# The fourth product of a maximum's scores with 64 rows instead of 32

## The chip, the cores and the metric

One core of one Trainium2 chip runs the whole program. The metric is the device time of one execution in microseconds, here 1030.96 us as the median of three runs (1029.35 to 1034.78). The core's engines work side by side and wait for each other by semaphores: PE (TensorE, the matmuls; PEld is its loading of weights), DVE (VectorE), ACT (ScalarE), POOL (GpSimd) and SP (SyncE, which issues nearly all DMAs).

## The reference

Attention with a decaying causal mask, then a layer of two products with a leaky ReLU between them, then a routed layer of eight experts. The change touches the attention alone, which for each of 4 batches and 8 heads (576 positions, 64 numbers each) computes

```
scores = q @ k.T / 8                      # 576 x 576
cum    = cumsum(log(clip(f)))             # one number per position
scores = where(later, -1e9, scores + cum[row] - cum[column])
scores = scores - max(scores, row)
attn   = exp(scores) / (sum(exp(scores), row) + 1e-9)
out    = attn @ v
```

The row's own `cum[row]` falls out of the softmax, so the kernel adds only `-cum[column]`.

## The kernel before, in words

The program has four stages. The first, up to about 300 us, is attention together with the first products of the next layer; then come the two halves of that layer's first product and its logits (to about 560 us), the second product with the routing, and the experts.

Attention goes by pairs of heads, 16 in all. A head's 64 numbers per position lie on 64 partitions, so one head of a pair has partitions 0 to 63 and the other 64 to 127, and each product is issued twice, for `u` in 0 and 1. Every float32 operand is split into a high and a low part, and three products (high by high, low by high, high by low) are added up in PSUM.

A fourth product adds what isn't q times k. For it there are two more tiles per set, `QR` and `KR` (three sets in turn, 640 columns each, lines 539 to 549). In each head's 64 partitions, `QR` has ones in rows 0 and 1 and the maxima of the rows (high and low part, brought by a DMA, line 715) in rows 32 and 33; `KR` has the two parts of `-cum` in rows 0 and 1 (a DMA, lines 610 to 612) and ones in rows 32 and 33. All other rows are zeros, from POOL's memsets at the start.

Each pair passes through three functions. `prepare` (line 554) loads k and q, transposes them on PE (tile `T`) and splits them on ACT and DVE. `offsets` (line 642) computes the scores once with the queries as weights, finds each row's maximum (DVE, `maximum`, line 666) and the sum of the exponentials (ACT, `total`, line 677). `attend` (line 738) computes the scores again, transposed, with the keys as weights, this time with the maximum subtracted by the fourth product, takes the exponential (ACT, tile `P`, line 771), zeroes what lies above the diagonal (POOL, line 775), and multiplies by v on PE (tile `av`).

The two kinds of score products look almost the same. In `offsets` the fourth product takes 32 rows, since the rows from 32 on of `QR` hold the maxima, which must not be added there; in `attend` it takes all 64:

```
661:  for m, (x, y, r) in enumerate(((qh, kh, 64), (ql, kh, 64), (qh, kl, 64), (qr, kr, 32))):
662:      for u in range(2):
663:          d = slice(64 * u, 64 * u + r)
664:          pe.matmul(p[:, u, a:a + c1 - c0], x[d, 128 * t:128 * t + 128], y[d, c0:c1], ...)

765:  for m, (x, y) in enumerate(((kh, qh), (kl, qh), (kh, ql), (kr, qr))):
766:      for u in range(2):
767:          d = slice(64 * u, 64 * u + 64)
```

Below, a score block of `offsets` is called a maximum's block. A pair has six of them (lines 703 to 707), 192, 64, 320, 448, 288 and 288 columns wide; the 192 and the 64 stand in one PSUM tile and follow each other directly. With 16 pairs that makes 96 blocks and 192 fourth products. In the profile a product's names are `s<-moving,weights`: `s<-kh,qh`, `s<-kh,ql`, `s<-kl,qh` and `s<-kr,qr 32*128` are the four of a maximum's block, `s<-qh,kh` to `s<-qr,kr 64*128` those of `attend`. `attend` has its blocks in four tiles: c (320 columns), a (448), b (320 and 192), d (256 and 64).

All score blocks share two PSUM buffers (tag `s`), taken in turn. A block may begin when the readers of the block two before it are done: two to four DVE instructions for a maximum's block, one ACT exponential for a tile of `attend`.

The order of the work is fixed when the program is built. Each operation of the stage is given to a planner (`Plan`, line 91) with an engine, an estimate of its time and a rank; the planner plays the engines through and writes down one order for each, which the engines then follow. The product of a maximum's block is planned with `2 * mm_ns(widths)` (line 681), the memsets with 560 or 100 ns (line 543 on); the first pair's come first on POOL (`pads`, rank `12 * n - 100`). Between the attention's products the planner puts, from the middle of the stage on, products of the next layer (`h`, line 875) and the preparation of its weights (tiles `w`, `wbits`, `wsq`, `wh`).

Of the kernel before, what the change touches and what calls it, by code (L numbers as in the profile page):

```python
# [12 lines left out]
FT = mybir.dt.float32  # L13
FR = mybir.dt.float32r
# [181 lines left out]
def tile_kernel(ctx, tc, q, k, v, f, w_in, w_out, w_gate, w1, w2, out):  # L196
# [4 lines left out]
    vec, act, pe, gp, sp = (InOrder(tc, x) for x in (V, A, PE, G, nc.sync))  # L201
# [279 lines left out]
    with ExitStack() as c1:  # L481
        stp_ = tc.tile_pool(name="sets", bufs=1, side="right", reuse_waits="tile")
        stp = stp_.__enter__()
# [16 lines left out]
        def mm_ns(*widths):  # L500

            last = widths[-1] / 2.4
            return 2 * sum(max(w / 2.4, 107) + 3 for w in widths) + (50 if last > 106 else last - 80)
# [33 lines left out]


        QH, QL, QR, KH, KL, KR = zip(*([stp.tile([128, W1], FR, name=f"{n}{i}") for n in ("qh", "ql", "qr", "kh", "kl", "kr")] for i in range(3)))
        pads = []  # L540
        for i in range(3):
            n = (i + 1) % 3
            fs = [(560, lambda i=i: gp.memset(QR[i].bitcast(FT), 0.0)), (560, lambda i=i: gp.memset(KR[i].bitcast(FT), 0.0))]
            for u in range(2):
                fs += [(560, lambda i=i, u=u: gp.memset(QR[i][64 * u:64 * u + 2].bitcast(FT), 1.0)),
                       (560, lambda i=i, u=u: gp.memset(KR[i][64 * u + 32:64 * u + 34].bitcast(FT), 1.0))]
            for x, c in ((QH, 0), (QL, 0), (KH, S), (KL, S)):
                fs.append((100, lambda x=x[i], c=c: gp.memset(x[:, c:c + 64].bitcast(FT), 0.0)))
            pads.append([op("gp", ns, fn, (), 12 * n - 100) for ns, fn in fs])
# [92 lines left out]
        def offsets(n, own, z):  # L642

            qh, ql, qr, kh, kl, kr = (x[(n + 2) % 3] for x in (QH, QL, QR, KH, KL, KR))
            kq = [own["k"], own["q"]]

            def tiles():
                own["nm"] = at.tile([128, 2, 6], FT, name="nm", tag="nm", bufs=2)
                own["sm"] = at.tile([128, 2, 6], FT, name="sm", tag="sm", bufs=2)
            mins, tots = [], []  # L650

            def part(ts, z, last):

                sc = {}

                def product():
                    if "nm" not in own:
                        tiles()
                    sc[0] = p = ps.tile([128, 2, 512], FT, name="s", tag="s", bufs=2)
                    for t, i, c0, c1, a in ts:  # L660
                        for m, (x, y, r) in enumerate(((qh, kh, 64), (ql, kh, 64), (qh, kl, 64), (qr, kr, 32))):
                            for u in range(2):
                                d = slice(64 * u, 64 * u + r)
                                pe.matmul(p[:, u, a:a + c1 - c0], x[d, 128 * t:128 * t + 128], y[d, c0:c1], start=m == 0, stop=m == 3)

                def maximum(u, t, i, c0, c1, a):

                    w, nm = c1 - c0, own["nm"]
                    own_keys = c1 == 64 + 128 * t
                    if a == 0:  # L670
                        sc["kept", u] = kept[plan.kept % NK]
                        plan.kept += 1
                    vec.tensor_tensor_reduce(out=sc["kept", u][:, a:a + w], in0=sc[0][:, u, a:a + w], in1=mask[:, 448 - w:] if own_keys else mask[:, :w], scale=-1.0,
                                             scalar=nm[:, u, 5:6] if i else 3e38, op0=OP.add, op1=OP.min,
                                             accum_out=nm[:, u, t:t + 1] if own_keys else nm[:, u, 5:6])

                def total(u, t, i, c0, c1, a):
                    x = sc["kept", u][:, a:a + c1 - c0]
                    act.activation(x, x, AF.Exp, bias=own["nm"][:, u, t:t + 1], scale=-1.0, accum_out=own["sm"][:, u, t + i:t + i + 1])
                first = "nmb" not in own  # L680
                o = op("pe", 2 * mm_ns(*(x[3] - x[2] for x in ts)), product, own["ready"] + ([own["tiles"]] if not first else []), z, ["s"] + ["nm", "sm"] * first,
                       kq + ([] if first else own["nmb"]))
                sb0 = o.got[0]
                if first:
                    own["tiles"], own["nmb"] = o, o.got[1:]
                nb, sb = own["nmb"]
                r = []
                for u in range(2):
                    ms, hold = [], []
                    for x in ts:  # L690
                        m = op("vec", 85 + 1.042 * (x[3] - x[2]), lambda u=u, x=x: maximum(u, *x), [o] + [y[0] for y in last[u:u + 1]], z + 1, ["kept"] if not hold else (), [sb0, nb] + hold)
                        hold = hold or m.got
                        ms.append(m)
                    mins.extend(ms)
                    r.append((ms[0], hold[0], lambda u=u: total(u, *ts[0])))
                    if ts[0][0] == 4 and ts[0][1] == 0:
                        continue
                    for x, m in zip(ts, ms):
                        tots.append(op("act", 280 + .833 * (x[3] - x[2]), lambda u=u, x=x: total(u, *x), [m], z + 2, (), hold + [nb, sb]))
                    if last:  # L700
                        tots.append(op("act", 280 + .833 * 288, last[u][2], [ms[0]], z + 2, (), [last[u][1], nb, sb]))
                return r
            part([(1, 0, 0, 192, 0), (0, 0, 0, 64, 192)], z, [])
            part([(2, 0, 0, 320, 0)], z + 2, [])
            part([(3, 0, 0, 448, 0)], z + 4, [])
            l = part([(4, 0, 0, S // 2, 0)], z + 6, [])
            part([(4, 1, S // 2, S, 0)], z + 8, l)

            def inverse():
                sm = own["sm"]  # L710
                vec.tensor_tensor(sm[:, :, 4], sm[:, :, 4], sm[:, :, 5], op=OP.add)
                vec.tensor_scalar(sm[:, :, :5], sm[:, :, :5], 1e-9, None, op0=OP.add)
                vec.reciprocal(sm[:, :, :5], sm[:, :, :5])
            nb, sb = own["nmb"]
            own["max"] = rows(lambda: own["nm"], lambda u: qr[64 * u + 32:64 * u + 34], mins, z + 12, [nb], kq)
            o = op("vec", 530, inverse, tots, z + 14, (), [sb])
            mine = {}

            def flip():
                mine[0] = ps.tile([128, 512], FT, name="T", tag="T", bufs=plan.depth["T"])  # L720
                pe.transpose(mine[0][:12, :128], own["sm"].rearrange("p u t -> p (u t)"), ident)

            def copy():
                mine[1] = at.tile([12, 128], FT, name="xi", tag="xi", bufs=2)
                act.copy(mine[1], mine[0][:12, :128])
            o = op("pe", 107, flip, [o], z + 15, ["T"], [sb])
            o = op("act", 158, copy, [o], z + 16, ["xi"], o.got)
            o = op("sp", 450, lambda: sp.dma_start(invd[n], mine[1]), [o], z + 17, (), o.got, 30)

            def spread(u):  # L730
                if u == 0:
                    own["R"] = at.tile([128, S], FT, name="R", tag="R", bufs=2)
                sp.dma_start(own["R"][64 * u:64 * u + 64], invd[n, 6 * u:6 * u + 5].rearrange("t q -> (t q)")[64:].partition_broadcast(64))
            a = op("sp", 625, lambda: spread(0), [o], z + 18, ["R"], (), 410)
            own["Rb"] = a.got[0]
            own["inv"] = [a, op("sp", 625, lambda: spread(1), [o], z + 18, (), a.got, 410)]
# [108 lines left out]
        for g in range(NA + 1):  # L845
# [9 lines left out]
            for j in range(NF if g < NA else 0):  # L855
                m, hb, o = {}, [], None
# [20 lines left out]
                a = op("act", 264, copy, [o], ZV, ["eg"] if j == 0 else (), hb + gb)  # L877
# [148 lines left out]
    with ExitStack() as c3:  # L1026
# [77 lines left out]
        for e in range(E):  # L1104
# [6 lines left out]
            for j in range(NJ):  # L1111
                for i in range(j, j + 2):
                    n, i = e + i // NJ, i % NJ
# [230 lines left out]
```

## Time and profile before

| | |
|---|---|
| median of three runs | 1030.96 us (1029.35 to 1034.78) |
| the profiled execution, its own time | 1028.66 us |
| its span from the first to the last instruction | 1026.9 us |
| PE busy in the span | 986.9 us (96%) |
| PEld, DVE, ACT, POOL busy | 79%, 56%, 42%, 43% |
| matmuls | 7939 |

The span is what the trace shows of the profiled execution; 1.8 us of its time lie around it. A matmul's recorded duration reaches past the start of the next, because products overlap; how much time one takes from PE is read from the distance of its start to the next one's. In the timeline, successive instructions of the same form are merged: a line with `x2` is the two products for `u` in 0 and 1, which start within a few ns of each other, and its time is the start of the first.

### The profile page before, as it was taken

The numbers are of one execution on the slowest core, as the hardware profiler recorded it, in microseconds if no ns is written. First come the engines' busy times: TensorE is split into PE (matmuls) and PEld (weight loads), VectorE is DVE, ScalarE is ACT, GpSimd is POOL, SyncE is SP. The second block draws the span as 40 slices with busy tenths as digits, with TensorE's granted clock in tenths as the row PEclk, the third lists the DMA queues.
The fourth block names the chain that finished last, engine by engine and source line by source line (L and its number), as shares of the span: only waits on it lengthen the run. The fifth ranks groups of instructions, "written<-read, shape, count | busy, mean of one in ns | idle before, by whom it ended". The sixth has DMA issues, their size and how long they took to land.

```text
span 1026.9 us, 21248 instructions
## 1 busy us (share of the span) xinstructions
PE 986.9 (96%) x7939; PEld 816.0 (79%) x7939; DVE 574.2 (56%) x1591; ACT 433.9 (42%) x1077; POOL 438.3 (43%) x563
## 2 busy tenths in 40 slices
PE   6999999999988999999999999999996999999996
PEld 4666666676677998899987777777675999999996
DVE  4577776444426786873353565445745565666541
ACT  4687777555532323342232222122332454555531
POOL 5267775222258784840043444444675221222011
PEclk9999999999998999999999999999998999999998
DMA  5265675342359974543232212122143656666521
GB/s 121 68 177 155 183 191 151 92 133 80 94 169 370 298 237 156 157 141 103 83 114 62 63 50 55 62 62 63 53 123 108 191 175 203 210 186 196 166 72 37
DMA packets 140809, 138.89 MB, mean 135 GB/s; under 512 B 69633, under 2 KB 98817, under 8 KB 140449
## 3 DMA queue, kind: packets, MB, share of 16 engines
q1 hardware_dynamic: 137632, 128.08, 41.3%
q0 software_dynamic: 3072, 9.44, 3.3%
q8 instruction: 62, 1.02, 0.4%
q14 instruction: 43, 0.34, 0.1%
HBM read 106.67 MB, written 30.65 MB: 134 GB/s over the span
## 4 chain that ended last, share of the span: by engine, by line
PE 78%; issue 9%; DVE 5%; POOL 3%; DMA 3%; ACT 2%; SPq 0%; POOLq 0%; ACTq 0%; DVEq 0%
PE h L60 19%; PE acc L1012 19%; PE s L60 13%; PE h L1068 6%; PE y L1081 6%; PE T L60 6%; PE av L60 5%; PE q_ct L1012 3%; POOL out L1089 1%; DMA X<-xd 1%; ACT kept L60 1%; PE T L1058 1%; DVE wbits L60 1%; DVE wh L60 1%; PE T L1086 1%
## 5 line engine op out<-in xcount | busy, mean ns | idle before, releaser
L60 PE MATMUL h<-X,wh 128*128 128x256 f32 x1728 | 232.5, 288 | 3.7 <-DVE g L60 2.1
L60 PEld LDWEIGHTS h<-X,wh 128*128 128x128 f32 x1728 | 212.1, 190 | 20.8 <-issue 9.4
L1012 PE MATMUL acc<-wh,gh 128*128 128x512 f32 x576 | 190.3, 404 | 0.0
L423 POOL TENSOR_TENSOR gl<-g,gh 128x512 fp32r<-128x512 f32 x72 | 96.5, 1342 | 111.3 <-ACT gh L422 100.1
L1012 PEld LDWEIGHTS acc<-wh,gh 128*128 128x128 f32 x576 | 109.4, 191 | 20.8
L60 ACT ACTIVATE g<-h 128x256 f32<-128x256 f32 x144 | 55.4, 385 | 162.1 <-PE h L60 156.2
L1068 PE MATMUL h<-XE,wh 128*128 128x288 f32 x768 | 118.5, 303 | 0.3 <-ACT XE L1059 0.3
L1012 PE MATMUL acc<-wh,gl 128*128 128x512 f32 x288 | 118.8, 413 | 0.0
L323 ACT CAST wh<-wst 128x512 fp32r<-128x512 f32 x132 | 79.9, 620 | 81.0 <-DMA wst<-in_moe_w 47.8
L60 DVE TENSOR_TENSOR wh<-wst,wh 128x512 fp32r<-128x512 f32 x132 | 90.6, 707 | 41.4 <-ACT wh L323 29.0
L422 ACT CAST gh<-g 128x512 fp32r<-128x512 f32 x72 | 44.5, 621 | 162.4 <-PE acc L1012 131.7
L60 ACT ACTIVATE kept<-kept,nm 128x192 f32<-128x192 f32 (+2 forms) x192 | 97.3, 508 | 29.4 <-DVE nm L60 28.1
L1068 PEld LDWEIGHTS h<-XE,wh 128*128 128x128 f32 x768 | 106.7, 191 | 0.6 <-ACT XE L1059 0.6
L60 DVE TENSOR_TENSOR g<-g,h 128x256 f32<-128x256 f32 x144 | 59.9, 417 | 76.7 <-ACT g L60 76.2
L1081 PE MATMUL y<-eh,wh 128*128 128x288 f32 x512 | 98.2, 296 | 0.3 <-issue 0.3
L60 DVE CUSTOM_DVE_ANT_0 kept<-s,mask 128x192 f32<-128x192 f32 (+4 forms) x160 | 61.6, 427 | 54.6 <-PE s L60 54.0
L1081 PEld LDWEIGHTS y<-eh,wh 128*128 128x128 f32 x512 | 79.5, 188 | 0.4 <-issue 0.4
L1089 POOL DMA_INDIRECT out<-yo,ids x24 | 24.4, 1019 | 129.7 <-DVE yo L1088 120.1
L60 PE MATMUL av<-P,vt 128*64 128x256 f32 (+4 forms) x512 | 68.5, 358 | 2.2 <-DVE R L60 1.8
L60 DVE SCALAR_TENSOR_TENSOR wbits<-w,wbits 128x256 int32<-128x256 int32 x128 | 68.7, 542 | 2.3
L1081 PE MATMUL y<-el,wh 128*128 128x288 f32 x256 | 67.7, 296 | 0.0
L60 POOL TENSOR_SCALAR_AFFINE_SELECT P<-P 128x256 f32<-128x256 f32 (+1 forms) x80 | 29.5, 386 | 85.0 <-ACT P L60 84.9
(195 smaller groups left out, 1665.1 us busy)
## 6 DMA issues: line engine op xcount, KB each, us to landing
wst<-in_moe_w SPq DMA_DIRECT2D x128, 256.0 KB
X<-xd SPq DMA_DIRECT2D x10, 1024.0 KB
gd<-g SPq DMA_DIRECT2D x36, 256.0 KB
g<-gd SPq DMA_DIRECT2D x36, 256.0 KB
w<-in_moe_w_in SPq DMA_DIRECT2D x32, 256.0 KB
w<-in_moe_w_out SPq DMA_DIRECT2D x32, 256.0 KB
xd<-xt SPq DMA_DIRECT2D x16, 320.0 KB
R<-invd SPq DMA_DIRECT2D x32, 144.0 KB
```

Source lines behind the costliest of these rows:

```text
L60: r = getattr(self.engine, name)(*a, **k)
L323: A.copy(r[u][0], x)
L422: A.copy(gh, g)
L423: G.tensor_tensor(gl, g, gh, op=OP.subtract)
L1012: tc.keep_in_program_order(PE.matmul(*a, **k))
L1058: PE.transpose(p[:, M * t:M * t + M], xe[t][:, 128 * c:128 * c + 128], ident[:M, :M])
L1068: PE.matmul(h[:, :CAP], w, X[:, c, x, :], start=n == 0, stop=n == 3 * NC - 1)
L1081: PE.matmul(yt[c][:, :CAP], w[:, s], a, start=j == 0 and n == 0, stop=j == NJ - 1 and n == 2)
L1086: PE.transpose(p[:M, 128 * c:128 * c + 128], ys[:, c, M * t:M * t + M], ident)
L1089: sd = G.indirect_dma_start(out=out[:, :], out_offset=bass.IndirectOffsetOnAxis(ap=ids[:, 3 * e + t:3 * e + t + 1], axis=0), in_=y, in_off ...
```

## The change

A constant tile `QO` of 128 by 128 has ones in rows 0 and 1 of each head's 64 partitions and zeros in the others. It takes the place of `QR` as the weights of a maximum's fourth product, which now reads 64 rows of `QO` and of `KR`: the ones that `KR` has in rows 32 and 33 meet zeros. `QO` is filled by three memsets on POOL, after the first two memsets of the first pair's set. `attend` is as before.

```
         QH, QL, QR, KH, KL, KR = zip(...)
+        QO = stp.tile([128, 128], FR, name="qo")
         pads = []
         for i in range(3):
             n = (i + 1) % 3
             fs = [(560, lambda i=i: gp.memset(QR[i].bitcast(FT), 0.0)), (560, lambda i=i: gp.memset(KR[i].bitcast(FT), 0.0))]
+            if n == 0:
+                fs += [(150, lambda: gp.memset(QO.bitcast(FT), 0.0))]
+                fs += [(150, lambda u=u: gp.memset(QO[64 * u:64 * u + 2].bitcast(FT), 1.0)) for u in range(2)]
...
                     for t, i, c0, c1, a in ts:
-                        for m, (x, y, r) in enumerate(((qh, kh, 64), (ql, kh, 64), (qh, kl, 64), (qr, kr, 32))):
+                        for m, (x, y) in enumerate(((qh, kh), (ql, kh), (qh, kl), (QO, kr))):
+                            q = slice(0, 128) if m == 3 else slice(128 * t, 128 * t + 128)
                             for u in range(2):
-                                d = slice(64 * u, 64 * u + r)
-                                pe.matmul(p[:, u, a:a + c1 - c0], x[d, 128 * t:128 * t + 128], y[d, c0:c1], start=m == 0, stop=m == 3)
+                                d = slice(64 * u, 64 * u + 64)
+                                pe.matmul(p[:, u, a:a + c1 - c0], x[d, q], y[d, c0:c1], start=m == 0, stop=m == 3)
```

## Rows read from the trace of the kernel before

**Rows 1.** Busy time in stretches (PE, PEld, DVE, ACT, POOL, clock, DMA share, GB/s)

```profile
58.12:72.95 14.83, 14.80 (x140) 10.04 (x141) 10.81 (x41) 11.16 (x35) 9.74 (x15) 1.00 0.57 158
182.25:204.78 22.53, 22.53 (x185) 16.13 (x184) 9.55 (x38) 12.38 (x37) 5.11 (x9) 1.00 0.37 103
```

**Rows 2.** PE's timeline, maximum's blocks of one pair (start us, duration, instruction)

```profile
58.42 0.28 PE L60 MATMUL s<-kl,qh 64*128 64x192 f32 x2
58.63 0.36 PE L60 MATMUL s<-kr,qr 32*128 32x192 f32 x2
58.92 0.30 PE L60 MATMUL s<-kh,qh 64*128 64x64 f32 x2
59.05 0.28 PE L60 MATMUL s<-kh,ql 64*128 64x64 f32 x2
...
60.26 0.31 PE L60 MATMUL s<-kl,qh 64*128 64x320 f32 x2
60.49 0.41 PE L60 MATMUL s<-kr,qr 32*128 32x320 f32 x2
60.83 0.28 PE L60 MATMUL T<-ident,sm 128*12 128x128 f32 x1
...
66.70 0.40 PE L60 MATMUL s<-kr,qr 32*128 32x288 f32 x2
67.02 0.53 PE L60 MATMUL T<-ident,x 128*128 128x128 f32 x2
```

**Rows 3.** PE's timeline, blocks b and d of attend

```profile
70.16 0.31 PE L60 MATMUL s<-ql,kh 64*128 64x320 f32 x2
70.31 0.31 PE L60 MATMUL s<-qr,kr 64*128 64x320 f32 x2
...
70.65 0.28 PE L60 MATMUL s<-ql,kh 64*128 64x192 f32 x2
70.77 0.27 PE L60 MATMUL s<-qr,kr 64*128 64x192 f32 x2
70.88 0.30 PE L60 MATMUL s<-qh,kh 64*128 64x256 f32 x2
...
71.37 0.20 PE L60 MATMUL s<-qh,kh 64*128 64x64 f32 x2
71.40 0.28 PE L60 MATMUL s<-qh,kl 64*128 64x64 f32 x2
```

**Rows 4.** PE's timeline, a 64-row fourth product with a 128-row product after it

```profile
141.53 0.31 PE L60 MATMUL s<-qr,kr 64*128 64x320 f32 x2
141.78 0.63 PE L60 MATMUL h<-X,wh 128*128 128x256 f32 x3
```

**Rows 5.** An exponential of attend, the block after it, and PEld's waits from 43 to 175 us

```profile
66.49 0.70 ACT L60 ACTIVATE P<-s 128x640 f32<-128x640 f32 x1
...
67.29 0.53 PE L60 MATMUL s<-qh,kh 64*128 64x448 f32 x2
...
PEld s L60 <- ACT P L60: 7.0, 17, 0.6
```

**Rows 6.** PE's timeline in the first 38 us, a maximum's block and one of attend

```profile
28.70 0.47 PE L60 MATMUL s<-kl,qh 64*128 64x320 f32 x2
29.10 0.63 PE L60 MATMUL s<-kr,qr 32*128 32x320 f32 x2
29.66 0.74 PE L60 MATMUL s<-kh,qh 64*128 64x448 f32 x2
...
35.93 0.47 PE L60 MATMUL s<-qr,kr 64*128 64x320 f32 x2
36.20 0.57 PE L60 MATMUL s<-qh,kh 64*128 64x448 f32 x2
```

**Rows 7.** POOL's timeline at the start, a memset of 128x128 and POOL's first work after the memsets

```profile
0.79 0.20 POOL masks.py:197 MEMSET ident<- 128x128 f32 x1 [0.29 <-POOLq L1331]
...
37.24 0.41 POOL L60 TENSOR_SCALAR_AFFINE_SELECT P<-P 128x256 f32<-128x256 f32 x1 [22.01 <-ACT P L60]
```

## The prediction, made before the changed kernel ran

> **What bounds the kernel now.** I looked first at the busy time in stretches of the attention stage, since the change touches that stage alone. For one pair in the stage's first half PE is busy 14.80 of 14.83 us, with ACT at 11.16, DVE at 10.81 and POOL at 9.74; for one in its second half, where products of the next layer fill in, PE is busy 22.53 of 22.53 us and no other engine over 12.4 [rows 1]. So PE bounds the stage. But a busy PE isn't PE at its pace: products overlap, so next I read its timeline by the distance from start to start.
>
> There the maximum's blocks stand out. In the 192-wide one the fourth product starts 0.21 us after the third, the next block's first product 0.29 us after that, and the second 0.13 us later [rows 2]. `attend` has the same widths with 64 rows throughout: 0.12 us from third to fourth, 0.11 to the next block, and 0.03 from first to second in a 64-wide block [rows 3]. In the 320-wide blocks it is 0.23 against 0.15 [rows 2, 3]. The widths, the pairing for `u` and the number of weight columns are the same; what differs is the rows. PE loses time when it goes from 64 rows to 32 and again when it leaves 32.
>
> Last I looked at what waits for what, because a faster PE is worth something only where no other engine holds the next product. PE has next to no idle time, but PEld waited 17 times for ACT's exponential before a score block [rows 5], so in places ACT arrives just in time.
>
> **The change part by part.** *The product.* It keeps its columns, its place and its readers; only its rows change, so I cost it by the steps of `attend`.
>
> - 192 followed by 64: 0.21 to 0.12, 0.29 to 0.11, 0.13 to 0.03: 0.09 + 0.18 + 0.10 = 0.37 us [rows 2, 3].
> - The 64-wide block: its entry as the 192-wide one's, 0.09; its exit I cost at nothing, having no wide product to shorten.
> - 320: entry 0.23 to 0.15, 0.08; exit to a 128-row product 0.34 [rows 2], against 0.25 after a 64-row fourth product of the same width [rows 4]: 0.09. Together 0.17.
> - 288, twice: the exit is 0.32 [rows 2]; there is no 64-row fourth product of that width, so it lies between nothing saved and the 0.09 of the 320-wide block; nearest is the latter. With the entry 0.17 each.
> - 448: taken as the 320-wide block, 0.17.
>
> That is 0.37 + 0.09 + 0.17 + 2 x 0.17 + 0.17 = 1.14 us of PE's time per pair at full clock.
>
> What of that lies on the path? In the first half, the exponential of tile c ran from 66.49 to 67.19, and the 448-wide block of `attend`, which takes a PSUM buffer from it, started at 67.29 [rows 5]. A 288-wide maximum's block stands between them. Its 0.17 us only makes PE arrive earlier at a wait that ACT ends, so it is lost: 0.97 us per pair stay. The other wait of that kind, of the next pair's first block for the exponential of tile b, is different: ACT comes to that exponential after the row sums, which come after DVE's maxima of the second 288-wide block, which come after PE's product. There everything shifts along.
>
> Of the 16 pairs I count in PE's timeline two in the first 43 us, nine of the first kind, four of the second, and one at the end, of the first kind again. The nine give 9 x 0.97 = 8.7 us. The four have PE work of the next layer to go on with, and PE doesn't wait: 4 x 1.14 = 4.6. The last gives 1.0.
>
> The first two ran at TensorE's lower clock: the step from one 320-wide block of `attend` to the next block is 0.27 us there, where the step from third to fourth is 0.15 later [rows 3, 6], so about the ratio of 1.2 to 2.4 GHz. There the 320-wide maximum's block has 0.40 before its fourth product and 0.56 after it, where `attend` has 0.27 after it [rows 6]; taking 0.27 for both, 0.13 + 0.29 = 0.42 us are lost, and with twice the 0.10 of the next block's first product, 0.62. In these two pairs five blocks have another 64-row block behind them and seven a 128-row product, which I put at 0.13 + 2 x 0.09, about 0.3, less for the 64-wide: 5 x 0.62 + 6 x 0.3, about 4.9. DVE has to follow, and the first block's fourth product waits for a DMA; I take 4.0, between 2 and 5.
>
> The sum is 8.7 + 4.6 + 1.0 + 4.0 = 18.3 us. Everything after the stage is issued behind it in program order, so its end moves the rest along.
>
> *The memsets.* Three more at the head of POOL's order, at most 0.2 us each by the 128 by 128 one of the start [rows 7], 0.6 us. The first use of `KR` and `QO` is covered by the loads, transposes and the DMA of `cum`, which the fourth product waits for anyway, and POOL's memsets are followed by 22 us of idleness [rows 7]. Cost nothing; 0.6 us if that cover were gone.
>
> *The waits.* The fourth product no longer reads `QR` and now reads rows 32 to 63 of `KR`, written only at the start. No wait is added after the first pair. *The order.* The planner's estimate of the product is unchanged; its POOL clock begins 0.45 us later on operations that nobody waits for, so I take the order to be the same. If it isn't, I allow 3 us either way: the few waits in the stage are of that size.
>
> The profiled execution took 1028.66 us, so the sum gives 1010.4. The median shown is 2.3 us above that execution; by the median it would be 1012.7. I say 1012.
>
> One rule bears on the exits. The profile first: leaving a 32-row product for a 128-row one takes 0.34 us, leaving a 64-row one 0.25 [rows 2, 4], so an exit is cheaper although both change the shape. The Trainium skill, in "TensorEngine Tiling (Array Packing)", section "Key Properties", says that changing the tiling mode drains TensorE; by it, 64 to 128 rows remains a change and this exit would save nothing. I go by the rows, and the other case is a rival below.
>
> **The rivals.**
>
> 1. *Each vanished switch saves its own price and an exit to 128 rows saves nothing.* Then a block saves its entry of 0.09 and only the 192-wide one 0.37: 0.37 + 5 x 0.09 = 0.82 us per pair, 0.73 on the path. 9 x 0.73 + 4 x 0.82 + 0.7 + 3 = 13.6 us: 1017. Against it stand the exits of rows 2 and 4. This is what the Trainium skill's rule would give ("TensorEngine Tiling (Array Packing)", "Key Properties").
> 2. *ACT, DVE and POOL take over in the nine pairs.* They are at 65 to 75% of a pair's 14.83 us [rows 1], and PEld already waits for ACT at places [rows 5]. If all of those 8.7 us turn into such waits, 9.6 stay: 1021. Against it: ACT's own waits there are mostly for products that now come earlier.
> 3. *The clock rises earlier.* At 36 us the steps are still those of the low level [rows 6], although PE has been at work. With fewer holes in PE's stream the rise might come some 7 us sooner; one us at the low level costs 1 - 0.15/0.27 = 0.44 us, so 3 us more: 1009.
> 4. *The clock falls (slower).* If PE, now faster, stands at the waits for ACT in each pair, and the clock drops there, each us at the low level costs 0.44 us by the same ratio. From 42 us on, some three of the thirteen pairs at full clock, the saving is eaten up; six such pairs, 89 us, would cost 39: 1051. Against it: waits of this size are there now, and the clock held.
> 5. *The change doesn't do what it says:* the price hangs on this fourth product for another reason than its rows, such as its operand coming from tiles written by DMA. Then 1031. Against it: `attend`'s fourth product reads the same two tiles, at the cheap steps.
>
> **How the numbers follow.** Forecast 0.62, rival 1 0.06, rival 2 0.13, rival 3 0.09, rival 4 0.05, rival 5 0.05. A measurement of this kernel can tell about 0.5%, 5 us, from no change. The forecast and rivals 1 to 3 are faster by more: 0.90. Rival 5 is the same, 0.05; rival 4 slower, 0.05. The range reaches down to rival 3 and the uncertain start, 1006, and up to rival 2, 1021, which leaves out rivals 4 and 5 and the edges of the others, under 2 in 10.
>
> **What would show it.** Right: the fourth product stands as a 64-row form with `qo`; 0.11 to 0.15 us from third to fourth; the 64-wide block's second product 0.03 after its first; exits to 128 rows near 0.25; a pair of the first kind takes about 13.9 us for 14.83, one of the second 21.4 for 22.53; the stage's last score block comes some 18 us sooner, and what follows has its length. Wrong: steps shortened but pairs not (rival 2, with idle time of PE before `s`), exits still at 0.34 (rival 1), entries still at 0.2 (rival 5), stretches of the stage with a granted clock under 1 (rival 4).

## The result, and the profile after

The changed kernel took 1003.83 us (median of four runs, 1003.01 to 1004.71) against 1030.15 for the kernel before on the same chip. The ratio is 0.9737, with a 95% interval of 0.9704 to 0.9771. Two later comparisons gave 0.9713 (0.9648 to 0.9778) and 0.9715 (0.9681 to 0.9749). It was forecast faster, at 1012 us with a range from 1006 to 1021: the direction and the price of the steps came true, the size didn't; the time lies 2 us under the range.

PE's timeline of one pair of the first kind in the changed kernel, in the columns of [rows 2] and [rows 3]:

```profile
64.85 0.27 PE L60 MATMUL s<-kl,qh 64*128 64x192 f32 x2
64.96 0.28 PE L60 MATMUL s<-kr,qo 64*128 64x192 f32 x2
65.08 0.21 PE L60 MATMUL s<-kh,qh 64*128 64x64 f32 x2
65.12 0.28 PE L60 MATMUL s<-kh,ql 64*128 64x64 f32 x2
...
66.22 0.32 PE L60 MATMUL s<-kl,qh 64*128 64x320 f32 x2
66.37 0.32 PE L60 MATMUL s<-kr,qo 64*128 64x320 f32 x2
66.62 0.27 PE L60 MATMUL T<-ident,sm 128*12 128x128 f32 x1
...
72.20 0.29 PE L60 MATMUL s<-kr,qo 64*128 64x288 f32 x2
72.42 0.53 PE L60 MATMUL T<-ident,x 128*128 128x128 f32 x2
72.85 0.47 PE L60 MATMUL s<-qh,kh 64*128 64x448 f32 x2
```

The fourth product is now a 64-row form with `qo`. In the 192-wide block it follows the third after 0.11 us (0.21 before), the next block follows after 0.12 (0.29), and its second product after 0.04 (0.13). In the 320-wide block the entry is 0.15 (0.23) and the exit to a 128-row product 0.25 (0.34); the exit of the 288-wide block is 0.22 (0.32). Up to the 320-wide block these are the steps of `attend` within 0.01 us ([rows 3], [rows 4]); a 288-wide block `attend` doesn't have.

Busy time in two stretches of the changed kernel, one pair of each kind, in the columns of [rows 1]:

```profile
50.58:64.55 13.97, 13.67 (x142) 9.70 (x142) 10.40 (x41) 11.43 (x35) 10.23 (x16) 1.00 0.58 164
185.76:207.16 21.40, 21.40 (x188) 15.62 (x186) 9.72 (x39) 12.49 (x38) 5.54 (x10) 1.00 0.44 117
```

A pair of the first kind takes 13.97 us for 14.83, one of the second 21.40 for 22.53. ACT's and DVE's work is about what it was, in less time. Where PE waits is seen in its waits from 36 to 165 us:

```profile
PE av L60 <- POOL P L60: 1.9, 6, 0.4
PE T L60 <- DVE xh L60: 0.5, 2, 0.3
PE s L60 <- ACT P L60: 0.5, 1, 0.5
```

Six times PE now stands before an `av` product until POOL has zeroed its part of `P`, 0.3 to 0.4 us each.

The marks below are starts of PE's instructions in the traces: the first product of the third, the twelfth and the sixteenth pair's maximum's blocks, and the last score product of the stage; then the low stretches of the clock at the start. The rows for the experiments come from the runs told in the next section.

| kernel | third | twelfth | sixteenth | last score | clock first high |
|---|---|---|---|---|---|
| before | 43.3 | 182.3 | 270.9 | 294.7 | from 38.0 |
| after | 36.4 | 164.5 | 249.9 | 272.4 | from 29.3 |
| order alone | 42.0 | 178.5 | 268.8 | 291.0 | from 37.3 |
| `QO` with 32 rows | 42.1 | 178.5 | 268.8 | 291.0 | from 37.5 |
| rows alone | 37.2 | 167.7 | 251.4 | 272.5 | 19.4 to 22.8, then from 29.7 |
| before, grouped | 41.4 | 177.3 | 264.5 | 286.5 | from 35.6 |
| before, extra products | 42.7 | 181.6 | 270.3 | 292.2 | 7.3 to 14.1, then from 38.0 |
| after, extra products | 32.1 | 160.4 | 245.8 | 266.8 | 7.3 to 21.0, then from 24.4 |

Of the 23.9 us between the two spans (1026.9 and 1003.0), 22.3 come in the attention stage, 6.9 of them before the third pair. Until its first recorded change the profile prints a granted clock of 1.00; that the clock is low there is read from the steps, 0.27 us and more as in [rows 6].

### The profile page after: what moved, and what is told of

Same layout as the page of the kernel before. It is cut to its first block, busy times and chain, and to the rows that moved or that the text cites. A ratio compares the mean times of both kernels' runs of the same rounds, so it can differ in the third digit from the quotient of the medians.

```text
span 1003.0 us, 21252 instructions
## 1 busy us (share of the span) xinstructions
PE 962.5 (96%) x7939; PEld 809.7 (81%) x7939; DVE 577.5 (58%) x1591; ACT 435.0 (43%) x1077; POOL 439.5 (44%) x566
## 4 chain that ended last, share of the span: by engine, by line
PE 75%; issue 10%; DVE 8%; POOL 4%; DMA 2%; ACT 1%; SPq 0%; POOLq 0%; ACTq 0%; DVEq 0%
PE h L60 20%; PE acc L1017 18%; PE s L60 9%; PE h L1073 7%; PE y L1086 6%; PE T L60 5%; PE av L60 5%; PE q_ct L1017 3%; DVE kept L60 1%; POOL out L1094 1%; DVE wbits L60 1%; PE T L1063 1%; DVE xh L60 1%; POOL xt L60 1%; POOL wsq L60 1%
## 5 line engine op out<-in xcount | busy, mean ns | idle before, releaser
L60 PEld LDWEIGHTS h<-X,wh 128*128 128x128 f32 x1728 | 212.6, 190 | 20.3 <-issue 10.9
L1017 PE MATMUL acc<-wh,gh 128*128 128x512 f32 x576 | 188.1, 400 | 0.0
L60 DVE TENSOR_TENSOR wh<-wst,wh 128x512 fp32r<-128x512 f32 x132 | 90.2, 707 | 37.8 <-ACT wh L323 29.9
L1017 PEld LDWEIGHTS acc<-wh,gl 128*128 128x128 f32 x288 | 54.4, 189 | 10.6 <-issue 2.0
```

The source lines that it names most:

```text
L60: r = getattr(self.engine, name)(*a, **k)
L1017: tc.keep_in_program_order(PE.matmul(*a, **k))
```

## The experiments

### Order, rows and tile taken apart

The order of PE's work in the changed kernel is not that of the kernel before: at the first pair the transposes of the next pair lie elsewhere between the score blocks, and later on some `h` products and transposes have moved. So the first question was how much of the gain is order. One kernel keeps the new tile, the memsets and the order, and gives the product its 32 rows back:

```
-for m, (x, y) in enumerate(((qh, kh), (ql, kh), (qh, kl), (QO, kr))):
-    q = slice(0, 128) if m == 3 else slice(128 * t, 128 * t + 128)
+for m, (x, y, r) in enumerate(((qh, kh, 64), (ql, kh, 64), (qh, kl, 64), (qr, kr, 32))):
     for u in range(2):
-        d = slice(64 * u, 64 * u + 64)
+        d = slice(64 * u, 64 * u + r)
```

> The changed kernel's tile, memsets and order of work, but the fourth product with QR's 32 rows as before. If the rows alone carry the gain: 1030 us, within 3, third to fourth product of a 192-wide block 0.20 us, the clock rising at about 38 us. If the new order carries what my sum was short of (some 6 us): about 1024.

It took 1026.05 us, a ratio of 0.9945 (0.9915 to 0.9974). The next one changes the rows alone: the three memsets stand ahead of the planned operations, and PE does the stage's work in the order of the kernel before.

```
         QO = stp.tile([128, 128], FR, name="qo")
+        gp.memset(QO.bitcast(FT), 0.0)
+        for u in range(2):
+            gp.memset(QO[64 * u:64 * u + 2].bitcast(FT), 1.0)
...
-            if n == 0:
-                fs += [(150, lambda: gp.memset(QO.bitcast(FT), 0.0))]
-                fs += [(150, lambda u=u: gp.memset(QO[64 * u:64 * u + 2].bitcast(FT), 1.0)) for u in range(2)]
```

> The changed product, but the three memsets stand ahead of the planned operations, so that the stage keeps the order of the kernel before. If the rows carry all: 1004, within 3, third to fourth product 0.11 us, the clock rising near 29 us. If the order carries 6 us of it: about 1010.

It took 1006.7 us, 0.9755 (0.9690 to 0.9819). The third has the constant tile but only 32 rows of it:

```
-        d = slice(64 * u, 64 * u + 64)
+        d = slice(64 * u, 64 * u + (32 if m == 3 else 64))
```

> The changed kernel with its constant tile as the weights, but only 32 rows of it and of KR. If the number of rows sets the price: as the order-alone kernel, 1030 within 3, third to fourth product 0.20 us. If it was the tile (QR, which memsets and DMAs write) and not the rows: as the changed kernel, 1004, third to fourth 0.11 us.

It took 1024.31 us, 0.9947 (0.9918 to 0.9976). PE's timeline of that kernel:

```profile
57.82 0.27 PE L60 MATMUL s<-kl,qh 64*128 64x192 f32 x2
58.02 0.36 PE L60 MATMUL s<-kr,qo 32*128 32x192 f32 x2
58.30 0.30 PE L60 MATMUL s<-kh,qh 64*128 64x64 f32 x2
58.44 0.28 PE L60 MATMUL s<-kh,ql 64*128 64x64 f32 x2
```

The same tile `qo` at the old steps, 0.20, 0.28 and 0.14: it is the rows, not what the weights are or where they come from. Both 32-row kernels came out faster than the 1027 to 1033 us expected if the rows carry all, so the order has a part too. The changed kernel ran beside these three.

> The changed kernel itself, beside the three, for the same chip: 1004 within 2 by every theory.

It took 1003.83 us again, 0.9713 (0.9648 to 0.9778).

So the rows carry nearly all. The order-alone kernel has the order of the changed one, the rows-alone kernel that of before, so each number of rows stands in both orders. By the medians the rows give 22.3 us in the order of before (1028.98 to 1006.7) and 22.2 in the new one (1026.05 to 1003.83), the order 2.9 us with either number of rows. With 32 rows that is half a per cent, clear of the noise; with 64 rows there are four runs of each kernel and they overlap, so a gain by the order isn't shown there.

Where the order's gain comes from can be read in the traces. PE's first fourth product, in the kernel before, in the order-alone kernel and in the changed one:

```profile
12.08 0.67 PE L60 MATMUL s<-kr,qr 32*128 32x192 f32 x2 [1.43 <-DMA kr<-cumd]
```

```profile
11.11 0.77 PE L60 MATMUL s<-kr,qr 32*128 32x192 f32 x2 [0.60 <-DMA kr<-cumd]
```

```profile
11.02 1.02 PE L60 MATMUL s<-kr,qo 64*128 64x192 f32 x2 [0.51 <-DMA kr<-cumd]
```

In the new order the wait for the DMA of `kr` ends 1.0 us sooner, with 32 rows as with 64, and the third pair of the order-alone kernel begins 1.2 us earlier than before (42.0 for 43.3). In the rows-alone kernel that product starts at 12.27. Later, twelve `h` products have gone from the eleventh pair to the fifteenth: with 32 rows the eleventh takes 15.3 us for 18.2 and the fifteenth 22.5 for 20.8, with 64 rows 14.3 for 17.1 and 21.3 for 19.6; why the first gains more than the second loses stays open. In their traces the two 64-row kernels reach the stage's end together (272.4 and 272.5 us), but in the changed kernel's last pair the clock is low for 3.4 us (264.8 to 268.2), about 1.5 us at 0.44 per us; a later trace of it without that stretch has its last score product at 271.4. The trace of before has such a stretch too, from 273.5 to 276.9, and those of the two 32-row kernels don't.

### Is the price paid per change of rows or per product?

This kernel is the one before, with the same 192 fourth products of 32 rows; but in the tile of the 192- and the 64-wide block the two are put side by side at the end, as one accumulation.

```
-for t, i, c0, c1, a in ts:
-    for m, (x, y, r) in enumerate(((qh, kh, 64), (ql, kh, 64), (qh, kl, 64), (qr, kr, 32))):
-        for u in range(2):
-            ...
+for ms in ((0, 1, 2), (3,)):
+    for t, i, c0, c1, a in ts:
+        for m in ms:
+            x, y, r = ((qh, kh, 64), (ql, kh, 64), (qh, kl, 64), (qr, kr, 32))[m]
+            for u in range(2):
+                ...  start=m == 0 and a == 0, stop=m == 3 and (t, i, c0, c1, a) == ts[-1]
```

> The kernel before, but in the tile of the 192- and the 64-wide block the two 32-row fourth products stand together at the end: as many 32-row products, one entry and one exit fewer per pair. If the price hangs on the change between 64 and 32 rows: 0.35 us less per pair, 6 us in all, 1023 against 1029. If it hangs on each 32-row product: no change, 1029 within 2.

It took 1020.47 us, 0.9903 (0.9871 to 0.9935). Its timeline:

```profile
56.19 0.28 PE L60 MATMUL s<-kl,qh 64*128 64x192 f32 x2
56.30 0.21 PE L60 MATMUL s<-kh,qh 64*128 64x64 f32 x2
56.35 0.28 PE L60 MATMUL s<-kh,ql 64*128 64x64 f32 x2
56.46 0.28 PE L60 MATMUL s<-kl,qh 64*128 64x64 f32 x2
56.67 0.41 PE L60 MATMUL s<-kr,qr 32*128 32x192 f32 x4
57.01 0.34 PE L60 MATMUL av<-P,vt 128*64 128x64 f32 x4
```

From the 192-wide third product to the next block it is 0.11 us, and 0.05 on; the change to 32 rows now comes once, 0.21 before the four 32-row products (the `x4`). A pair of the first kind takes 14.5 us for 14.83 (55.88 to 70.37, its first product and the next pair's), 0.34 less, where 0.35 was expected. The time went down by 8.7 us between the medians, about as the stage (294.7 to 286.5), of which 1.5 may again be that low stretch, which this trace doesn't have either, and 1.9 come before the third pair; the 6 expected are there. The price is paid per change of rows.

The Trainium skill says in "TensorEngine Tiling (Array Packing)", section "Key Properties", that changing the tiling mode drains TensorE. With the entries and with this run the trace agrees, as far as a price at each change goes; a drain itself no run here shows. Taken as one fixed price for any change it doesn't hold: going to a 128-row product is a change from 32 rows and from 64, and from start to start it took 0.34 and 0.25 us behind the 320-wide fourth product.

### The clock at the start

15 products of a constant bf16 tile, whose results nothing reads, are put where PE waits: 10 ahead of everything, 2 before the second set of transposes, 3 before the first fourth product. They go into both kernels alike.

```
+        wz = stp.tile([128, 512], BF, name="wz")
+        V.memset(wz, 1.0)
+        wv = ps.tile([128, 512], FT, name="av", tag="av", bufs=1)
+        def fill(k):
+            for _ in range(k):
+                pe.matmul(wv, wz[:, :128], wz, start=True, stop=True)
+        fill(10)
...
```

> The kernel before, with 15 products of a constant bf16 tile that nothing reads, on PE before its first work (10) and in two of its waits in the first 12 us (2 and 3). If PE's inactivity at the start holds the clock low: the clock rises before 25 us instead of at 38, and some 13 us at the high level give 4 to 6 us: 1024. If it is the 32-row blocks that keep it low: it falls again at the first ones or doesn't rise, 1029 within 2.

> The changed kernel with the same 15 products. If the start of the changed kernel still loses to the clock: the rise comes before 20 us instead of at 29 and the time falls by 3 to 5 us, to 1000. If the earlier rise in the changed kernel gave nothing, since DVE and ACT bound the start: 1004 within 2.

The kernel before took 1027.5 us with them, 0.9988 (0.9961 to 1.0015): nothing. Its busy time in four stretches of the start (columns of [rows 1]; the clock is the last but two):

```profile
7.40:14.00 6.60, 4.90 (x35) 2.78 (x34) 2.10 (x9) 2.44 (x6) 6.32 (x14) 1.00 0.66 155
14.20:21.00 6.80, 6.80 (x32) 4.25 (x30) 3.85 (x18) 4.96 (x19) 0.88 (x5) 0.50 0.64 145
21.20:24.20 3.00, 2.03 (x9) 1.07 (x9) 1.95 (x8) 1.82 (x8) 0.00 (x0) 0.50 0.21 47
24.60:37.80 13.20, 13.20 (x70) 8.76 (x69) 5.72 (x26) 7.39 (x26) 0.41 (x1) 0.50 0.20 52
```

and the same stretches of the changed kernel with the 15 products:

```profile
7.40:14.00 6.60, 5.33 (x41) 3.35 (x42) 3.36 (x16) 3.69 (x12) 6.34 (x15) 1.00 0.60 136
14.20:21.00 6.80, 5.43 (x56) 4.04 (x54) 5.05 (x23) 6.55 (x25) 1.48 (x6) 1.00 0.64 144
21.20:24.20 3.00, 2.99 (x20) 2.48 (x18) 2.54 (x15) 2.50 (x12) 0.00 (x0) 0.50 0.04 10
24.60:37.80 13.20, 13.12 (x131) 9.01 (x129) 7.82 (x36) 11.19 (x37) 3.74 (x7) 1.00 0.56 133
```

In both the clock was high (1.00, the 2.4 GHz level) from 7.3 us. With 32-row blocks it fell at 14.1 us to the 1.2 GHz level and stayed there for 24 us, although PE is busy throughout 14.2 to 21.0 and 24.6 to 37.8. With 64-row blocks it stayed up until 21.0, fell for 3.4 us after a stretch with a wait (5.43 of 6.80 busy), and was back from 24.4 on. These two kernels differ in their order too: in the first PE waited for its first fourth product until 12.11 us, in the second that product ran at 11.00. So that the fall at 14.1 belongs to the rows isn't shown. What the rows do to the rise is shown by the kernels without extra products: with the order of before it comes at 38.0 us with 32 rows and at 29.7 with 64, after a short high stretch from 19.4 to 22.8; with the new order at 37.3 and 37.5 with 32 rows and at 29.3 with 64. In the changed kernel it comes during the transposes behind a maximum's block, before the first block of `attend`:

```profile
27.46 0.44 PE L60 MATMUL s<-kh,qh 64*128 64x288 f32 x2
27.70 0.44 PE L60 MATMUL s<-kh,ql 64*128 64x288 f32 x2
27.94 0.44 PE L60 MATMUL s<-kl,qh 64*128 64x288 f32 x2
28.18 0.44 PE L60 MATMUL s<-kr,qo 64*128 64x288 f32 x2
28.55 0.38 PE L60 MATMUL T<-ident,sm 128*12 128x128 f32 x1
28.73 1.20 PE L60 MATMUL T<-ident,x 128*128 128x128 f32 x5
29.85 0.41 PE L60 MATMUL s<-qh,kh 64*128 64x320 f32 x2
30.10 0.31 PE L60 MATMUL s<-qh,kl 64*128 64x320 f32 x2
```

The changed kernel with 15 products took 1001.3 us, 0.9731 (0.9681 to 0.9781); its stage ended 5.6 us sooner (266.8 for 272.4). Whether that reaches the whole time was tried once more beside the changed kernel, together with one that has 2 more products ahead of the first 448-wide block and 5 more ahead of the third pair's first transposes:

```
+                    if t0 == 0 and (n, j) in ((0, 1), (2, 0)):
+                        fill(5 if n else 2)
...
+                            if n == 0 and (m, t) in ((3, 1), (0, 3)):
+                                fill(3 if m else 2)
```

> The changed kernel once more, as the measure for the next two on the same chip: 1004 within 2.

> The changed kernel with the 15 products again: if the earlier clock is worth something in the whole time as it is in the stage (its last score block came 5.6 us sooner), 999 to 1001, below the changed kernel; if later work gives it back, 1003 to 1004.

> The same with 2 more products ahead of the first 448-wide block and 5 more ahead of the third pair's first transposes, where the profile shows waits of 0.6 and 1.4 us. If these waits brought the clock down again from 21.0 to 24.4 us: no low stretch there and 1.5 us less than with 15. If not: the same, or up to 1 us more where the products come in the way.

They took 1002.29, 1001.89 and 1000.75 us, ratios 0.9715 (0.9681 to 0.9749), 0.9715 (0.9683 to 0.9748) and 0.9710 (0.9677 to 0.9743). In the last one the low stretch from 21.0 to 24.4 is gone:

```profile
21.20:24.20 3.00, 2.60 (x23) 1.58 (x19) 2.93 (x15) 2.82 (x14) 0.00 (x0) 1.00 0.11 27
```

and the last score product comes at 265.8 us, against 271.4 in the changed kernel of the same chip. But the three whole times can't be told apart, and in the second one the low stretch was longer (19.9 to 26.7). In the traces nothing behind the stage gives the gain back: from the last score product to the end it is 732.3, 731.4 and 732.5 us. But the profiled execution of the changed kernel was the slowest of its six (1005.40), that of the last one its second fastest (999.97), so the 5.6 us between their stages can't be taken for the gain; a further gain from these products isn't shown.

## Why the prediction was wrong in size

**The price of a block.** Right. Entry 0.08 to 0.10, exits 0.09 to 0.10, the 192-to-64 passage 0.36, next to 0.08 and 0.09, 0.09 and 0.37 as costed. Rival 1, by which an exit to a 128-row product saves nothing, is out by the exits of after; rival 5, another cause than the rows, by the kernel with `QO` at 32 rows.

**What of it lies on the path.** Right. The nine pairs of the first kind were put at 8.7 us: in the rows-alone kernel, whose order is that of before, they gave 138.97 - 130.54 = 8.4. The four of the second kind were put at 4.6 and gave 88.6 - 83.7 = 4.9. Rival 2, that ACT, DVE and POOL take over, didn't come; the new waits for POOL are 1.9 us in all. In the changed kernel the 448-wide block of `attend` starts 0.43 us after the transposes behind the 288-wide block (72.42 to 72.85), where it was 0.27 [rows 2, 5]: there the saving is spent on waiting, as foreseen.

**The start.** Here the sum failed. The first two pairs were put at 4.0; they gave 6.1 us in the rows-alone kernel and 6.9 in the changed one. Two marks of the order-alone kernel, which does the work in the order of the changed one:

```profile
32.16 0.38 PE L60 MATMUL T<-ident,sm 128*12 128x128 f32 x1
...
42.04 0.36 PE L60 MATMUL s<-kh,qh 64*128 64x192 f32 x2
```

In the changed kernel these products start at 28.55 and 36.38. The first mark comes 3.6 us sooner, and up to there both run at the low clock: the price of the steps, put at 4.0, was sized well enough. (One reading behind it was off: six blocks, not five, have another 64-row block behind them, which makes the sum 5.5 for 4.9.) Up to the second mark it is 2.0 more, 1.7 of them over transposes and blocks of `attend`, ahead of any other maximum's block. That is the clock, which the sum left where it stood: its earlier rise was a rival to the forecast instead of a term of it. The rise came 8.7 us earlier than before, up to 3.8 us at 0.44 per us; but what counts is the same work: from the first mark on the order-alone kernel is low for 5.1 us more, the changed one for 0.7, and 4.4 x 0.44 = 1.9. The other 1.2 us of the 6.9 come from the order.

**The last pair.** Put at 1.0, it gave 2.8 in the rows-alone kernel: 23.84 us from its first product to the last score product became 21.07. The trace of before has a low stretch of 3.4 us there, 1.5 us at 0.44; in the changed kernel, which also has one, the saving is 1.3.

**The order.** "I take the order to be the same" is the other step that failed: 0.45 us more on operations that nobody waits for moved PE's work in the first pair and later on. In the traces that is 1.2 us at the start, where the DMA of `kr` comes sooner, and 0.8 by the moved `h` products: in the changed kernel the nine pairs gave 10.9 us and the four 3.3, where the rows alone gave 8.4 and 4.9. The 3 us allowed either way cover it.

**The reference.** The sum by the profiled execution gave 1010.4; the forecast was put 1.6 us above it for a median of three runs. With 11 to 19 runs that median came out at 1028.98 to 1030.29.

Together: 1.6 us from the reference, 22.3 - 18.3 = 4.0 from the stage (2.0 from the clock and 2.0 from the order; the other differences cancel), 1.6 behind the stage, and 0.9 by which the profiled execution of after lies above its median, make 8.1 of the 8.2 us between 1012 and 1003.83. The stage's parts come from one trace of each kernel. The 1.6 behind the stage can't be laid to the change: the profile of before has two low stretches of the clock there, 3.4 us each at 532.9 and 744.5, that the first profile of after lacks; two later profiles of the changed kernel have them, at 510 and 722 us, and need 731.4 and 732.3 us from the last score product to the end, as before (732.2).

Rival 3, an earlier clock, came true with the forecast and not instead of it, at 2.0 us for the 3 that it had. Rival 4, a falling clock, didn't come.

## What to carry to other kernels

Among products that follow each other on PE, a different number of rows is a price of its own: here about 0.1 us on the way in and 0.1 to 0.3 on the way out, 0.9 us in a pair of 14.8 and 1.1 in one of 22.5. It is read from start to start, by setting one form beside a like form elsewhere in the same trace; widening a product with zeros takes it away, putting the odd ones side by side a part of it. Where PE is busy without a gap and its steps still show the low clock, an edit that makes the stream denser can bring the rise forward: give that a term of the sum, counted on the work that would still run at the low clock. And compare the planned orders before taking them to be the same.

## What was not expected of the hardware

In the kernel before with the extra products PE was busy 13.20 of 13.20 us, from 24.6 to 37.8, at a granted 0.50. The Trainium skill, in "TensorE: Matmul & The Clock Gate", section "Why this matters for your kernels", warns of idle gaps between bursts of matmuls; in that stretch there were none. With 64 rows instead of 32 in one product of four the rise came some 8 us earlier, in kernels of the same order and without extra products (29.7 for 38.0, 29.3 for 37.3). The busy share doesn't show what the rows cost, for a record covers it: the 192-wide fourth product of 32 rows lasts 0.36 us, and the next block starts after 0.29 [rows 2].
